# Priority for PSUM copies, gating and splits in an attention and gated-projection stage, and w_out decoded in four parts over four slots

## The chip, the cores and the metric

The kernel runs on one core of one Trainium2 chip. The metric is the device time of one execution in microseconds (us). TensorE is called PE (its weight loads PEld), VectorE DVE, ScalarE ACT, GpSimd POOL, and SyncE, which issues most transfers, SP.

## The reference

Three layers are computed one after the other in float32 (8 batches, 8 heads, 576 tokens, head size 64, so 4608 tokens of 512 features):

```python
# attention within chunks of 64 tokens
scores = scale * q_c @ k_c.T; attn = softmax(scores); x = attn @ v_c      # heads side by side: (B, S, 512)
# gated projection
gate = sigmoid(sum_k conv_w[k] * x shifted by k)                         # 5 taps along the tokens
x = (gate * (x @ w_val)) @ w_out
# feed-forward with layer norm
xn = (x - mu) / sqrt(var + 1e-6) * g_ln
out = x + relu(xn @ w_ch1) @ w_ch2
```

The weights arrive as float64, so the kernel decodes them from pairs of 32-bit words. Each float32 product is made of three matmuls on a high and a low part (hi*hi, hi*lo, lo*hi).

## The kernel before

**Units and blocks.** Attention goes by 36 units of 128 tokens, the gated projection by nine blocks of 512 tokens (four units). `slot(u)` writes, in this order: the loads of unit u+2 on SP, `a1(u)` (transposes of k and q on PE into two PSUM buffers of the pool `ps_t`, each copied out by ACT as `kT` and `qT`), the dense work of the slot's first half, `a4(u-2)` (transposes of the softmax result `pr`, copied out as `pT`), `a3(u)` (scores `sc` on PE; maximum `mx`, difference `ex`, sum `sm`, reciprocal and product `pr` on DVE, the exponential on ACT), `a5(u-2)` (product with v into `x`; ACT copies it twice, as `xf` and as the high part `xh`; POOL makes the low part `xl`), and the dense work of the second half.

**Dense work of a block.** `conv` makes the gate's argument `cg` (one ACT pass and four DVE passes per feature tile), `sigm` takes one sigmoid over the whole block on ACT, with a table load before it and another when the exponential comes back. `val(j, f)` runs twelve matmuls into `psv`, one of two PSUM buffers of the pool `ps_d`. DVE multiplies it with the gate into `gv`, which frees the buffer, ACT rounds `gv` to the high part `gh`, DVE takes the low part `gl`. `proj(j, t)` runs twelve matmuls on `gh`, `gl` and the split of w_out (`oh`, `ol`) into `pso`, which ACT copies to `y` and sends to DRAM. I call the four `val` chains of a block V#1 to V#4. V#3 needs the buffer that the `gv` of V#1 frees.

**Decode.** `split_w("o")` decodes w_out in four pieces: an ACT pass (line 107), three DVE passes (lines 108, 109, 110; the tile `da`, of which there are three), the high part on ACT (line 115) and the low part on POOL (line 116). It is written in slot 5. The feed-forward weights go the same way later (`split_ff`, called by `prep` after the last slot), some of them early, in gaps of the attention stage.

**What sets the order.** Each engine works through its own queue in order. A scheduler orders these queues when the program is built: work that is written earlier has the better priority, and work with nothing in its way is pulled forward into gaps. Only PE is kept in written order, in slots 0 to 6 and in the second half of the feed-forward.

Of the kernel before, what the change touches and what calls it, by code (L numbers as in the profile page):

```python
# [19 lines left out]
def tile_chunk_attention_gated_mlp(ctx: ExitStack, tc: tile.TileContext, q, k, v, w_val, conv_w, w_out, g_ln, w1, w2, out):  # L20
    nc = tc.nc
# [15 lines left out]
    CT = DM // P  # L37
# [28 lines left out]
    pD1 = s_d.enter_context(tc.tile_pool(name="pD1", bufs=1))  # L66
# [8 lines left out]
    y_dram = [dram.tile([BLK, DM], F32, name=f"yd{j}") for j in range(NB)]  # L75
# [36 lines left out]
    def split(hi, lo, raw, pool=None):  # L112
        a = (pool or stg).tile([P, DM], F32, tag="da", name="da", bufs=3)
        decode(raw, a)
        nc.scalar.activation(out=hi, in_=a, func=ACTF.Copy)
        nc.gpsimd.tensor_tensor(out=lo, in0=a, in1=hi, op=ALU.subtract)
        return a

    wv = {}

    def load_w(w, nm, slot0):
        raws = []
        for c in range(CT):
            raw = wA.tile([P, DM, 2], U32, tag=f"s{slot0 + c}", name="raw")
            nc.sync.dma_start(out=raw, in_=w[c * P:(c + 1) * P])
            raws.append(raw)
        wv[nm] = raws

    def split_w(nm):
        hs, ls = [], []  # L130
        for c, raw in enumerate(wv[nm]):
            hi = pD1.tile([P, DM], F32R, name=f"{nm}h{c}")
            lo = pD1.tile([P, DM], F32R, name=f"{nm}l{c}")
            split(hi, lo, raw)
            hs.append(hi)
            ls.append(lo)
        wv[nm] = (hs, ls)

    w1s, w2s, wraw = {}, {}, {}

# [29 lines left out]
    kT, qT, pt, pT = {}, {}, {}, {}  # L170

    def transpose_in(u, src, dst, nm):
        a = src.pop(u)
        t = pA.tile([P, NP, UN], F32, tag=nm, name=nm)
        ps = ps_t.tile([P, NP, UN], F32, tag="t", name="pst")
        for hp in range(NP):
            nc.tensor.transpose(out=ps[:, hp, :], in_=a[:, hp].rearrange("p r d -> p (r d)"), identity=ident)
        nc.scalar.activation(out=t, in_=ps, func=ACTF.Copy)
        dst[u] = t

    def a1(u):
        transpose_in(u, kr, kT, "kT")
        transpose_in(u, qr, qT, "qT")
# [30 lines left out]
    def a4(u):  # L214
        pr = pt.pop(u)
        t = pA.tile([P, NP, P], F32, tag="pT", name="pT")
        ps = ps_t.tile([P, NP, P], F32, tag="t", name="pst")
        for hp in range(NP):
            nc.tensor.transpose(out=ps[:, hp, :], in_=pr[:, hp].rearrange("p r k -> p (r k)"), identity=ident)
        nc.scalar.activation(out=t, in_=ps, func=ACTF.Copy)  # L220
        pT[u] = t

    xf, xh, xl = {}, {}, {}

    def new_block(j):
        o = boundary(j)
        t = pD2.tile([P, CT, BLK + 2 * HALO], F32, tag="xf", name="xf")
        if j == 0:
            nc.gpsimd.memset(t[:, :, 0:HALO], 0.0)
        else:  # L230
            ob = boundary(j - 1)
            e = BLK + (HALO if ob < BLK else 0)
            nc.gpsimd.tensor_copy(out=t[:, :, 0:HALO], in_=xf[j - 1][:, :, e:e + HALO])
        if o < BLK:
            nc.gpsimd.memset(t[:, :, HALO + o:2 * HALO + o], 0.0)
        xf[j] = t
        xh[j] = pD2.tile([P, CT, BLK], F32R, tag="xh", name="xh")
        xl[j] = pD2.tile([P, CT, BLK], F32R, tag="xl", name="xl")

    def a5(u):  # L240
        t = pT.pop(u)
        j, uu = divmod(u, UPB)
        va = vr.pop(u)
        x = ps_x.tile([P, 2, NP, UN], F32, tag="x", name="x")
        for i in range(NP // 2):
            for c in range(2):
                for f in range(2):
                    for r in range(2):
                        r0, o0 = CH * r, CH * f
                        nc.tensor.matmul(  # L250
                            out=x[o0:o0 + CH, r, i, c * CH:(c + 1) * CH],
                            lhsT=va[r0:r0 + CH, c, 2 * i + f, :],
                            rhs=t[r0:r0 + CH, 2 * i + f, c * CH:(c + 1) * CH],
                            start=True, stop=True,
                        )
        x = x[:, :, 0:NP // 2, :]
        if uu == 0:
            new_block(j)
        o = boundary(j)
        a, b = uu * UN, (uu + 1) * UN  # L260
        segs = [(max(a, lo), min(b, hi), sh) for lo, hi, sh in ((0, o, HALO), (o, BLK, 2 * HALO)) if max(a, lo) < min(b, hi)]
        for lo, hi, sh in segs:
            dst = xf[j][:, :, lo + sh:hi + sh].rearrange("p (r i) t -> p r i t", r=2)
            nc.scalar.activation(out=dst, in_=x[:, :, :, lo - a:hi - a], func=ACTF.Copy)
        for lo, hi, sh in segs:
            src = xf[j][:, :, lo + sh:hi + sh]
            dst = xh[j][:, :, lo:hi].rearrange("p (r i) t -> p r i t", r=2)
            nc.scalar.activation(out=dst, in_=x[:, :, :, lo - a:hi - a], func=ACTF.Copy)  # L268
            nc.gpsimd.tensor_tensor(out=xl[j][:, :, lo:hi], in0=src, in1=xh[j][:, :, lo:hi], op=ALU.subtract)  # L269


    cg = pD1.tile([P, CT, BLK + HALO], F32, name="cg")
# [17 lines left out]
    gh, gl = {}, {}  # L290

    def chain(ps, ops):
        n = len(ops)
        for i, (lt, rh) in enumerate(ops):
            nc.tensor.matmul(out=ps, lhsT=lt, rhs=rh, start=(i == 0), stop=(i == n - 1))  # L295

    def val(j, f):
        hs, ls = wv["v"]
        fs = slice(f * P, (f + 1) * P)
        ps = ps_d.tile([P, BLK], F32, tag="d", name="psv")  # L300
        ops = []
        for c in range(CT):
            ops += [(hs[c][:, fs], xh[j][:, c, :]), (hs[c][:, fs], xl[j][:, c, :]), (ls[c][:, fs], xh[j][:, c, :])]
        chain(ps, ops)
        o = boundary(j)
        gv = pD2.tile([P, BLK], F32, tag="gv", name="gv")
        for lo, hi, sh in ((0, o, 0), (o, BLK, HALO)):
            if lo < hi:
                nc.vector.tensor_tensor(out=gv[:, lo:hi], in0=ps[:, lo:hi], in1=cg[:, f, lo + sh:hi + sh], op=ALU.mult)  # L309
        a = pD1.tile([P, BLK], F32R, tag=f"gh{f}", name="gh")  # L310
        b = pD1.tile([P, BLK], F32R, tag=f"gl{f}", name="gl")
        nc.scalar.activation(out=a, in_=gv, func=ACTF.Copy)  # L312
        nc.vector.tensor_tensor(out=b, in0=gv, in1=a, op=ALU.subtract)  # L313
        gh[j, f], gl[j, f] = a, b

    def proj(j, t):
        hs, ls = wv["o"]
        ts = slice(t * P, (t + 1) * P)
        ps = ps_d.tile([P, DM], F32, tag="d", name="pso")
        ops = []  # L320
        for f in range(CT):
            ops += [(gh[j, f][:, ts], hs[f]), (gh[j, f][:, ts], ls[f]), (gl[j, f][:, ts], hs[f])]
        chain(ps, ops)
        y = pD2.tile([P, DM], F32, tag="y", name="y")
        nc.scalar.activation(out=y, in_=ps, func=ACTF.Copy)
        nc.scalar.dma_start(out=y_dram[j][ts, :], in_=y)

# [321 lines left out]
    def at(u, pos, fn):  # L651
        dense.setdefault((u + pos[0], pos[1]), []).append(fn)

    for j in range(NB):
        u = UPB * (j + 1) + LAG - 1
# [9 lines left out]
        for t in range(BLK // P):  # L665
            at(u, [(4, 0), (4, 1), (5, 0), (6, 0)][t], lambda j=j, t=t: proj(j, t))
    at(0, (4, 1), lambda: load_w(w_out, "o", CT))
    at(0, (5, 1), lambda: split_w("o"))
    for u in range(3, NU + LAG + 6):
        if u == MANUAL:  # L670
            head.close()
# [43 lines left out]
    for s in range(NS):  # L715
        for p in range(NPR):
# [3 lines left out]
            if s + 1 < NS and 2 <= p < 6:  # L720
                i = 2 * (p - 2)
# [30 lines left out]
```

## Time and profile before

| what | value |
|---|---|
| median of 3 runs | 1196.09 us (1195.82 to 1197.68) |
| the profiled execution | 1193.61 us, of which its span 1191.8 us |
| busy share of PE, DVE, ACT, POOL | 94%, 62%, 44%, 13% |
| mean granted clock of PE | 0.977 of 2.4 GHz |

The page gives shares over the whole span; the attention and projection stage takes the first 380 us of it, and a change there is read from the rows of that stage. A row of the timeline gives the start, the duration, the engine, the line, the operation and its tiles, and in brackets how long the engine had been idle and what ended that.

### The profile page before, as it was taken

Reading aid. Unit: us, or ns where it says so; the run is one execution under the profiler, and the core shown is the slowest. Engines: PE = TensorE matmul, PEld = TensorE weight load, DVE = VectorE, ACT = ScalarE, POOL = GpSimd, SP = SyncE. Lnnn points to the kernel's source line nnn. Section 1 sums busy time; section 2 is a strip of 40 time slices with the busy share of each in tenths; the row PEclk is TensorE's granted clock in tenths of the full one; section 3 lists DMA queues with packets and bytes.
Section 4 is the critical chain, followed back from the end, with each engine's and each line's share of the span. In section 5 each row is a group of like instructions: output and inputs, shape, how many; then the busy total and the mean of one; then the engine's idle time right before and its main releaser. Section 6 shows DMA issues by size and latency. Waiting matters only on the chain.

```text
span 1191.8 us, 18298 instructions
## 1 busy us (share of the span) xinstructions
PE 1114.5 (94%) x7128; PEld 902.3 (76%) x7128; DVE 738.2 (62%) x1237; ACT 527.4 (44%) x972; POOL 158.1 (13%) x160
## 2 busy tenths in 40 slices
PE   7859999899999688789999999999999999999998
PEld 6747777777777566568888878888788887878876
DVE  6878899988894985644564753534835436442433
ACT  4557678676666564333443323332413424221221
POOL 2221133111211433322221000000000000000000
PEclk8979999999999999989999999999999999999999
DMA  7655676655113673233333353332532332622212
GB/s 182 172 114 131 166 190 182 176 148 131 45 63 126 213 248 119 98 133 124 142 124 106 126 194 105 106 124 89 198 120 89 124 106 98 223 86 89 89 36 79
DMA packets 168860, 155.37 MB, mean 130 GB/s; under 512 B 120622, under 2 KB 128838, under 8 KB 168774
## 3 DMA queue, kind: packets, MB, share of 16 engines
q1 hardware_dynamic: 163590, 144.76, 39.7%
q10 hardware_dynamic: 5184, 9.44, 2.1%
q8 instruction: 56, 0.92, 0.3%
q14 instruction: 30, 0.25, 0.1%
HBM read 116.41 MB, written 37.75 MB: 129 GB/s over the span
## 4 chain that ended last, share of the span: by engine, by line
PE 61%; DVE 26%; ACT 5%; issue 3%; SPq 2%; DMA 1%; POOL 1%; DVEq 0%; POOLq 0%; ACTq 0%
PE acc L501 14%; PE x L526 14%; PE psf L501 14%; PE zy L526 9%; DVE cg L281 8%; PE psv L295 3%; DVE da L109 2%; DVE pr L211 2%; DVE da L110 2%; PE pso L295 2%; DVE sm L208 2%; PE psh L295 2%; DVE ex L202 1%; PE pst L369 1%; DVE mx L199 1%
## 5 line engine op out<-in xcount | busy, mean ns | idle before, releaser
L544 DVE TENSOR_TENSOR c<-x,c 128x512 f32<-128x512 f32 x96 | 66.1, 689 | 231.5 <-ACT c L540 175.1
L501 PE MATMUL acc<-w,h 128*128 128x512 f32 x768 | 186.0, 391 | 0.0
L501 PE MATMUL psf<-w,h 128*128 128x512 f32 x768 | 186.0, 391 | 0.0
L501 PEld LDWEIGHTS acc<-w,h 128*128 128x128 f32 x768 | 144.2, 188 | 31.4
L501 PEld LDWEIGHTS psf<-w,h 128*128 128x128 f32 x768 | 144.2, 188 | 31.3
L526 PE MATMUL x<-t,wc 128*128 128x512 f32 x576 | 149.4, 395 | 4.6 <-DVE c L544 4.2
L540 ACT ACTIVATE c<-zy 128x512 f32<-128x512 f32 x96 | 57.9, 603 | 195.2 <-PE zy L526 195.2
L526 PEld LDWEIGHTS x<-t,wc 128*128 128x128 f32 x576 | 109.3, 190 | 29.6 <-DVE c L544 5.1
L535 ACT ACTIVATE h<-c 128x512 fp32r<-128x512 f32 x96 | 60.5, 631 | 135.8 <-DVE c L544 135.2
L281 DVE SCALAR_TENSOR_TENSOR cg<-xf,cw,cg 128x516 f32<-128x516 f32 (+1 forms) x176 | 116.3, 707 | 0.8 <-ACT cg L279 0.6
L506 DVE TENSOR_TENSOR yt<-psf,yt 128x512 f32<-128x512 f32 x128 | 88.0, 689 | 23.8 <-PE psf L501 19.7
L526 PE MATMUL zy<-b,wc 128*128 128x512 f32 x384 | 100.1, 397 | 0.0
L526 PEld LDWEIGHTS zy<-b,wc 128*128 128x128 f32 x384 | 72.1, 190 | 14.9
L536 DVE SCALAR_TENSOR_TENSOR h<-c,h 128x512 fp32r<-128x512 f32 x96 | 68.0, 709 | 13.1 <-ACT h L535 12.7
L269 POOL TENSOR_TENSOR xl<-xf,xh 128x512 fp32r<-128x512 f32 (+1 forms) x40 | 50.3, 1260 | 154.1 <-ACT xh L268 153.9
L295 PE MATMUL psv<-xh,vh 128*128 128x512 f32 x144 | 60.3, 419 | 7.1 <-DVE gv L309 6.1
L411 POOL TENSOR_TENSOR wc<-raws,wc 128x256 fp32r<-128x256 f32 x56 | 48.4, 885 | 132.5 <-ACT wc L410 132.4
L295 PE MATMUL pso<-oh,gh 128*128 128x512 f32 x144 | 60.1, 417 | 5.6 <-ACT gh L312 5.1
L295 PE MATMUL psv<-xl,vh 128*128 128x512 f32 x144 | 57.5, 399 | 0.9 <-POOL xl L269 0.9
L295 PE MATMUL pso<-oh,gl 128*128 128x512 f32 x144 | 56.9, 397 | 0.7 <-DVE gl L313 0.7
L295 PE MATMUL psv<-xh,vl 128*128 128x512 f32 x144 | 57.4, 398 | 0.0
L526 PE MATMUL zy<-t,wc 128*128 128x512 f32 x192 | 50.6, 399 | 7.0 <-ACT t L410 3.9
(114 smaller groups left out, 1777.7 us busy)
## 6 DMA issues: line engine op xcount, KB each, us to landing
wc<-wc SPq DMA_DIRECT2D x112, 512.0 KB, 3.2
raw<-in_moe_w_ch SPq DMA_DIRECT2D x32, 512.0 KB, 5.0
yr<-yd SPq DMA_DIRECT2D x48, 256.0 KB, 3.0
vr<-in_v SPq DMA_DIRECT2D x144, 64.0 KB, 2.6
yd<-y ACTq DMA_DIRECT2D x36, 256.0 KB, 2.5
kr<-in_k SPq DMA_DIRECT2D x64, 128.0 KB, 2.9
qr<-in_q SPq DMA_DIRECT2D x64, 128.0 KB, 3.0
out<-yt SPq DMA_DIRECT2D x20, 256.0 KB, 3.1
```

The source lines that it names most:

```text
L109: nc.vector.scalar_tensor_tensor(out=au, in0=hw, scalar=0x80000000, in1=au, op0=ALU.bitwise_and, op1=ALU.bitwise_or)
L269: nc.gpsimd.tensor_tensor(out=xl[j][:, :, lo:hi], in0=src, in1=xh[j][:, :, lo:hi], op=ALU.subtract)
L281: nc.vector.scalar_tensor_tensor(out=o, in0=x[:, f, i + lo:i + hi], scalar=cw[:, i * CT + f:i * CT + f + 1], in1=o, op0=ALU.mult, op1=ALU.add,
L295: nc.tensor.matmul(out=ps, lhsT=lt, rhs=rh, start=(i == 0), stop=(i == n - 1))
L411: eng.tensor_tensor(out=lo, in0=a, in1=hi, op=ALU.subtract)
L501: nc.tensor.matmul(out=ps, lhsT=lt, rhs=rh, start=(g == 0 and k == 0 and (first or half)), stop=(g == 1 and k == 2 and (last or half)),)
L506: nc.vector.tensor_tensor(out=yt[i], in0=ps, in1=yt[i], op=ALU.add)
L526: nc.tensor.matmul(out=ps, lhsT=lt, rhs=rh, start=(start and c == 0 and i == 0), stop=(c == 1 and i == 2), skip_group_check=True)
L535: nc.scalar.activation(out=t[:, 0, :], in_=src, func=ACTF.Relu)
L536: nc.vector.scalar_tensor_tensor(out=t[:, 1, :], in0=src, scalar=0.0, in1=t[:, 0, :], op0=ALU.max, op1=ALU.subtract)
L540: nc.scalar.activation(out=t, in_=zy, func=ACTF.Copy)
L544: nc.vector.tensor_tensor(out=t, in0=x, in1=t, op=ALU.add)
```

## The change

The copies of `kT`, `qT`, `pT`, the whole of `xf`/`xh`/`xl`, the gating (`gv`, `gh`, `gl`) and the copy and transfer of `y` are written inside `tc.high_priority()`, so that the scheduler takes them before other work that is ready. `split_w` takes a range of pieces, and the four pieces of w_out are asked for in slots 5, 6, 7 and 8 instead of all in slot 5.

```diff
-    def split_w(nm):
-        hs, ls = [], []
-        for c, raw in enumerate(wv[nm]):
+    def split_w(nm, c0=0, c1=CT):
+        hs, ls = wv.setdefault(nm + "s", ([], []))
+        for c, raw in list(enumerate(wv[nm]))[c0:c1]:
...
     def transpose_in(u, src, dst, nm):
...
-        nc.scalar.activation(out=t, in_=ps, func=ACTF.Copy)
-        dst[u] = t
+        with tc.high_priority():
+            nc.scalar.activation(out=t, in_=ps, func=ACTF.Copy)
+            dst[u] = t
...
     def a5(u):
...
+        with tc.high_priority():
+            for lo, hi, sh in segs:
...
+                nc.scalar.activation(out=dst, in_=x[:, :, :, lo - a:hi - a], func=ACTF.Copy)
...
     def val(j, f):
...
+        with tc.high_priority():
+            for lo, hi, sh in ((0, o, 0), (o, BLK, HALO)):
+                if lo < hi:
+                    nc.vector.tensor_tensor(out=gv[:, lo:hi], in0=ps[:, lo:hi], in1=cg[:, f, lo + sh:hi + sh], op=ALU.mult)
...
+            nc.scalar.activation(out=a, in_=gv, func=ACTF.Copy)
+            nc.vector.tensor_tensor(out=b, in0=gv, in1=a, op=ALU.subtract)
...
     def proj(j, t):
...
+        with tc.high_priority():
+            nc.scalar.activation(out=y, in_=ps, func=ACTF.Copy)
+            nc.scalar.dma_start(out=y_dram[j][ts, :], in_=y)
...
-    at(0, (5, 1), lambda: split_w("o"))
+    for c in range(CT):
+        at(0, (5 + c, 1), lambda c=c: split_w("o", c, c + 1))
```

Where DVE's queue comes to the end of the convolution of block 0 (`cg` is that convolution, `da` the decode of w_out, `sm` and `pr` the softmax). Before, up to the last `cg`:

```order
L110 SCALAR_TENSOR_TENSOR da<-raw,da 128x512
L109 SCALAR_TENSOR_TENSOR da<-raw,da 128x512
L208 TENSOR_REDUCE sm<-ex_143 128x8
L110 SCALAR_TENSOR_TENSOR da<-raw,da 128x512
L209 RECIPROCAL sm<-sm 128x8
L281 SCALAR_TENSOR_TENSOR cg<-xf,cw,cg 128x256
L211 TENSOR_TENSOR pr<-ex_143,sm 128x512
L281 SCALAR_TENSOR_TENSOR cg<-xf,cw,cg 128x256
L199 TENSOR_REDUCE mx<-sc 128x8
L281 SCALAR_TENSOR_TENSOR cg<-xf,cw,cg 128x256
L202 TENSOR_TENSOR ex_144<-sc,mx 128x2x4x64
L281 SCALAR_TENSOR_TENSOR cg<-xf,cw,cg 128x256
```

And in the changed kernel, on the same engine around the last `cg` of block 0 and on to the first `gv`:

```order
L283 SCALAR_TENSOR_TENSOR cg<-xf,cw,cg 128x256
L108 TENSOR_SCALAR da<-da 128x512
L283 SCALAR_TENSOR_TENSOR cg<-xf,cw,cg 128x256
L208 TENSOR_REDUCE sm<-ex_143 128x8
L283 SCALAR_TENSOR_TENSOR cg<-xf,cw,cg 128x256
L209 RECIPROCAL sm<-sm 128x8
L109 SCALAR_TENSOR_TENSOR da<-raw,da 128x512
L211 TENSOR_TENSOR pr<-ex_143,sm 128x512
L110 SCALAR_TENSOR_TENSOR da<-raw,da 128x512
L108 TENSOR_SCALAR da<-da 128x512 x2
L109 SCALAR_TENSOR_TENSOR da<-raw,da 128x512 x2
L312 TENSOR_TENSOR gv<-psv,cg 128x512 x2
```

Before, all twelve decode passes of w_out stand ahead of the last `cg`. Now four do (one piece and the first pass of the second), six stand between it and the first `gv`, and the last two after that.

ACT's queue at the same place, before (`cg` at line 288 is the sigmoid of block 0):

```order
L107 ACTIVATE da<-raw 128x512
L206 ACTIVATE ex_143<-ex_143 128x8x64
L178 ACTIVATE kT<-pst 128x512
L115 ACTIVATE oh_762<-da 128x512
L178 ACTIVATE qT<-pst 128x512
L220 ACTIVATE pT<-pst 128x512
L115 ACTIVATE oh_771<-da 128x512
L264 ACTIVATE xf<-x 128x4x128
L268 ACTIVATE xh<-x 128x4x128
L206 ACTIVATE ex_144<-ex_144 128x8x64
L288 ACT_TABLE_LOAD
L288 ACTIVATE cg<-cg 128x4x512
```

And in the changed kernel, from the same pass of the decode on:

```order
L107 ACTIVATE da<-raw 128x512
L206 ACTIVATE ex_143<-ex_143 128x8x64
L178 ACTIVATE kT<-pst 128x512
L290 ACT_TABLE_LOAD
L290 ACTIVATE cg<-cg 128x4x512
L178 ACTIVATE qT<-pst 128x512
L221 ACTIVATE pT<-pst 128x512
L115 ACTIVATE oh_859<-da 128x512
L315 ACTIVATE gh<-gv 128x512 x2
L115 ACTIVATE oh_991<-da 128x512
L266 ACTIVATE xf<-x 128x4x128
L178 ACTIVATE kT<-pst 128x512
```

The sigmoid moved ahead of seven passes, among them the exponential of the next unit.

ACT's queue around the sigmoid of a later block (block 2), before:

```order
L288 ACT_TABLE_LOAD
L288 ACTIVATE cg<-cg 128x2064
L206 ACT_TABLE_LOAD
L206 ACTIVATE ex_144<-ex_144 128x8x64
L312 ACTIVATE gh<-gv 128x512
L264 ACTIVATE xf<-x 128x4x128
L268 ACTIVATE xh<-x 128x4x128
L312 ACTIVATE gh<-gv 128x512
L178 ACTIVATE kT<-pst 128x512
L178 ACTIVATE qT<-pst 128x512
L220 ACTIVATE pT<-pst 128x512
```

And in the changed kernel:

```order
L290 ACT_TABLE_LOAD
L290 ACTIVATE cg<-cg 128x2064
L266 ACTIVATE xf<-x 128x4x128
L270 ACTIVATE xh<-x 128x4x128
L206 ACT_TABLE_LOAD
L206 ACTIVATE ex_144<-ex_144 128x8x64
L178 ACTIVATE kT<-pst 128x512
L178 ACTIVATE qT<-pst 128x512
L315 ACTIVATE gh<-gv 128x512 x2
L221 ACTIVATE pT<-pst 128x512
```

The same ten passes stand ahead of `pT`, but `xf`, `xh`, `kT` and `qT` now come before both `gh`. From the last projection of block 8 on, no engine's queue differs.

## Rows read from the trace of the kernel before

**Rows 1.** Busy time by stage: us, PE, PEld, DVE, ACT, POOL, PEclk, DMA

```profile
48.00:84.00 36.00, 22.17 (x258) 17.36 (x258) 29.02 (x48) 20.19 (x37) 9.71 (x9) 0.72 0.68 170
84.00:345.00 261.00, 244.95 (x2823) 196.71 (x2823) 231.38 (x385) 185.05 (x306) 53.51 (x52) 0.99 0.51 134
...
400.00:465.00 65.00, 48.13 (x202) 38.01 (x202) 56.42 (x109) 39.04 (x89) 28.86 (x23) 0.92 0.66 215
```

**Rows 2.** Waits of PE in 48 to 84 us: total, times, longest

```profile
PE pst L219 <- ACT kT L178: 10.2, 2, 6.4
PE sc L192 <- ACT qT L178: 1.8, 1, 1.8
```

**Rows 3.** Timeline of PE, 77 to 87 us, first and last matmuls of V#3 and V#4

```profile
77.27 0.78 PE L295 MATMUL psv<-xh,vh 128*128 128x512 f32 x1
...
82.01 0.39 PE L295 MATMUL psv<-xh,vl 128*128 128x512 f32 x1
...
83.82 0.50 PE L295 MATMUL psv<-xh,vh 128*128 128x512 f32 x1
...
86.47 0.39 PE L295 MATMUL psv<-xh,vl 128*128 128x512 f32 x1
```

**Rows 4.** Timeline of DVE, 54 to 77 us

```profile
54.64 0.68 DVE L199 TENSOR_REDUCE mx<-sc 128x8 f32<-128x512 f32 x1
...
58.06 0.41 DVE L108 TENSOR_SCALAR da<-da 128x512 uint32<-128x512 uint32 x1
58.40 0.68 DVE L110 SCALAR_TENSOR_TENSOR da<-raw,da 128x512 uint32<-128x512 uint32 x1
59.00 0.68 DVE L109 SCALAR_TENSOR_TENSOR da<-raw,da 128x512 uint32<-128x512 uint32 x1
...
60.00 1.75 DVE L110 SCALAR_TENSOR_TENSOR da<-raw,da 128x512 uint32<-128x512 uint32 x1
...
72.21 0.47 DVE L281 SCALAR_TENSOR_TENSOR cg<-xf,cw,cg 128x256 f32<-128x256 f32 x1
...
73.71 0.20 DVE L209 RECIPROCAL sm<-sm 128x8 f32<-128x8 f32 x1
73.95 0.69 DVE L211 TENSOR_TENSOR pr<-ex,sm 128x512 f32<-128x512 f32 x1
76.20 1.29 DVE L309 TENSOR_TENSOR gv<-psv,cg 128x512 f32<-128x512 f32 x2 [1.56 <-ACT cg L288]
```

**Rows 5.** Timeline of POOL, the low part of the first w_out piece

```profile
59.82 1.38 POOL L116 TENSOR_TENSOR ol<-da,oh 128x512 fp32r<-128x512 f32 x1 [2.56 <-ACT oh L115]
```

**Rows 6.** Timeline of ACT, 63 to 76 us

```profile
63.38 0.58 ACT L178 ACTIVATE kT<-pst 128x512 f32<-128x512 f32 x1
...
72.97 1.28 ACT L288 ACT_TABLE_LOAD   x1
74.26 1.91 ACT L288 ACTIVATE cg<-cg 128x2048 f32<-128x2048 f32 x1
```

**Rows 7.** Busy time from one block's sigmoid start to the next, columns as rows 1

```profile
74.26:109.93 35.67, 32.86 (x384) 26.89 (x385) 25.82 (x41) 22.72 (x36) 4.08 (x4) 0.89 0.40 102
109.93:145.70 35.77, 34.34 (x403) 27.50 (x402) 29.83 (x50) 24.92 (x41) 5.92 (x6) 1.00 0.67 168
145.70:183.70 38.00, 35.05 (x398) 27.77 (x397) 36.75 (x60) 28.86 (x50) 11.60 (x11) 0.96 0.70 180
...
220.50:257.32 36.82, 33.69 (x401) 27.30 (x400) 34.06 (x58) 25.13 (x43) 5.62 (x7) 1.00 0.64 172
```

**Rows 8.** Waits of PE in 84 to 345 us: total, times, longest

```profile
PE psv L295 <- DVE gv L309: 6.1, 4, 2.8
PE pso L295 <- ACT gh L312: 4.8, 5, 2.1
PE pst L219 <- ACT kT L178: 2.1, 4, 0.6
```

**Rows 9.** Timeline of ACT, `pT` in the slot after the sigmoid of block 1

```profile
117.05 0.60 ACT L220 ACTIVATE pT<-pst 128x512 f32<-128x512 f32 x1 [0.26 <-PE pst L219]
```

More of the change, by code (lines that the diff above doesn't have):

```diff
@@ L136, in split_w @@
             ls.append(lo)
-        wv[nm] = (hs, ls)
     w1s, w2s, wraw = {}, {}, {}
@@ L219, in a4 @@
             nc.tensor.transpose(out=ps[:, hp, :], in_=pr[:, hp].rearrange("p r k -> p (r k)"), identity=ident)
-        nc.scalar.activation(out=t, in_=ps, func=ACTF.Copy)
-        pT[u] = t
+        with tc.high_priority():
+            nc.scalar.activation(out=t, in_=ps, func=ACTF.Copy)
+            pT[u] = t
     xf, xh, xl = {}, {}, {}
@@ L261, in a5 @@
         segs = [(max(a, lo), min(b, hi), sh) for lo, hi, sh in ((0, o, HALO), (o, BLK, 2 * HALO)) if max(a, lo) < min(b, hi)]
[L262 to L269, printed above, removed]
+        with tc.high_priority():
+            for lo, hi, sh in segs:
+                dst = xf[j][:, :, lo + sh:hi + sh].rearrange("p (r i) t -> p r i t", r=2)
+                nc.scalar.activation(out=dst, in_=x[:, :, :, lo - a:hi - a], func=ACTF.Copy)
+            for lo, hi, sh in segs:
+                src = xf[j][:, :, lo + sh:hi + sh]
+                dst = xh[j][:, :, lo:hi].rearrange("p (r i) t -> p r i t", r=2)
+                nc.scalar.activation(out=dst, in_=x[:, :, :, lo - a:hi - a], func=ACTF.Copy)
+                nc.gpsimd.tensor_tensor(out=xl[j][:, :, lo:hi], in0=src, in1=xh[j][:, :, lo:hi], op=ALU.subtract)
     cg = pD1.tile([P, CT, BLK + HALO], F32, name="cg")
@@ L297, in val @@
     def val(j, f):
-        hs, ls = wv["v"]
+        hs, ls = wv["vs"]
         fs = slice(f * P, (f + 1) * P)
@@ L306, in val @@
         gv = pD2.tile([P, BLK], F32, tag="gv", name="gv")
[L307 to L313, printed above, removed]
+        with tc.high_priority():
+            for lo, hi, sh in ((0, o, 0), (o, BLK, HALO)):
+                if lo < hi:
+                    nc.vector.tensor_tensor(out=gv[:, lo:hi], in0=ps[:, lo:hi], in1=cg[:, f, lo + sh:hi + sh], op=ALU.mult)
+            a = pD1.tile([P, BLK], F32R, tag=f"gh{f}", name="gh")
+            b = pD1.tile([P, BLK], F32R, tag=f"gl{f}", name="gl")
+            nc.scalar.activation(out=a, in_=gv, func=ACTF.Copy)
+            nc.vector.tensor_tensor(out=b, in0=gv, in1=a, op=ALU.subtract)
         gh[j, f], gl[j, f] = a, b
     def proj(j, t):
-        hs, ls = wv["o"]
+        hs, ls = wv["os"]
         ts = slice(t * P, (t + 1) * P)
@@ L324, in proj @@
         y = pD2.tile([P, DM], F32, tag="y", name="y")
-        nc.scalar.activation(out=y, in_=ps, func=ACTF.Copy)
-        nc.scalar.dma_start(out=y_dram[j][ts, :], in_=y)
+        with tc.high_priority():
+            nc.scalar.activation(out=y, in_=ps, func=ACTF.Copy)
+            nc.scalar.dma_start(out=y_dram[j][ts, :], in_=y)
     p2 = {}
```

## Prediction

> **What bounds the kernel now.** I read the busy time by stage first. From 84 to 345 us PE is busy 244.95 of 261 us, so there PE itself is the limit and at most 16 us can be won. Just before, from 48 to 84 us, PE is busy only 22.17 of 36 us and is granted 0.72 of 2.4 GHz, while DVE is busy 29.02 [rows 1]. That is the one place of the stage with a large hole. The list of waits names it: PE stands 10.2 us in two gaps, the longer 6.4, before the transposes of `pr`, because a `ps_t` buffer has not been emptied by the copy `kT` [rows 2]. V#3 starts right after the second gap, at 77.27 [rows 3]. The copy is not slow (0.58 us); it stands in ACT's queue behind the sigmoid, which runs from 74.26 to 76.17 [rows 6]. The sigmoid needs the last `cg`, which DVE finishes at 72.21 + 0.47 = 72.68, and V#3 needs the sigmoid too, through the first `gv` at 76.20 [rows 4]. So the end of the hole is set by DVE's queue ahead of the last `cg`, and in that queue stand all twelve decode passes of w_out. A second stretch is not PE-bound: from 400 to 465 us PE is busy 48.13 of 65 us and DVE 56.42 [rows 1].
>
> **The change part by part.** The instructions are the same in number and kind; only their order moves.
>
> *The first sigmoid.* In the changed order, from the first decode pass to the last `cg`, DVE has one L109 and one L110 (0.68 each), two L108 (0.41), `mx`, `ex` and `sm` (0.68 each, by the `mx` row) and six `cg` (0.47) [rows 4]: 1.36 + 0.82 + 2.04 + 2.82 = 7.0 us. It starts at 55.3, where DVE was through with the earlier `cg` and the `mx` (54.64 + 0.68); the `mx` now comes later, but the exponential before it also does. That gives 62.3. Two things can add to it. The exponential stands on ACT behind the fourth L107, which needs the `da` tile that POOL's first `ol` frees. And a DVE pass beside a POOL pass can grow: the L110 at 60.00 took 1.75 instead of 0.68 us while POOL worked from 59.82 to 61.20 [rows 4, 5]. I allow 0.7 us for the two together: the last `cg` ends at 63, with bounds 62 and 64.4 (two such passes), against 72.68.
>
> ACT can load the table meanwhile, so the sigmoid (1.91) ends near 65 [rows 6]. But DVE first does what now stands between: a reciprocal and `pr` (0.20 + 0.69), two L108, and four passes of L109 and L110, 0.9 + 0.82 + 2.72 = 4.4 us [rows 4]. So `gv` starts at 67.4, its first half takes 0.65 [rows 4], and V#3 can start at 68, or at 69.1 if one more pass meets POOL. Before it started at 77.27 [rows 3].
>
> From V#3 to V#4 before, 83.82 - 77.27 = 6.55 us went by, of which 82.40 - 77.27 = 5.1 were V#3 itself [rows 3]. Now `x`, which stands between the two, waits for `pT`, and `pT` stands on ACT behind both `gh`, two parts of the w_out split, five copies and exponentials (eight passes of 0.58), a table load (1.28) and another exponential [rows 6]. From the first `gv` on that is 4.6 + 1.3 + 0.6, and 0.6 for `pT` itself: 68 + 7.1 = 75.1. With `x`, some half of the 1.4 us that were left between V#3 and V#4, V#4 starts at 76. Against 83.82 this is a **gain of 7.8 us**. The bounds: 10 if V#3 and what ACT does behind it go at the best of these rows (V#4's matmuls are 0.24 us apart, V#3's 0.43 [rows 3]) and nothing holds `pT`; 4 if three further DVE passes meet POOL (3 x 1.07). What hides the moved passes: in the block after the first sigmoid DVE is idle for 35.67 - 25.82 = 9.85 us [rows 7], and the decode passes now behind the last `cg` cost 0.82 + 6 x 0.68 = 4.9. If that cover were gone, they would cost 4.9 us.
>
> On the clock: V#3's matmuls were spaced at 0.43 us behind the 6.4 us gap, V#4's at 0.24 [rows 2, 3]. The Trainium skill (TensorE: Matmul & The Clock Gate, HAM oscillation) says that idle gaps of PE throttle it, and that it stays at full rate if they are kept short. The trace agrees as far as its one long gap goes. By that rule the shorter gaps of the new order could leave V#3 at 2.4 GHz, and the gain would be nearer to 10 than to 7.8.
>
> *Slots 3 to 7.* `xh` moves ahead of the exponential, and the transposes of `pr` ahead of V#1. PE may reach the end of V#2 some 1 us earlier or later, but then it waits for `kT` all the same. I count 0, bounds -1 and +1.
>
> *The later blocks.* A block without much decode takes 35.8 us with PE busy 34.3 [rows 7]. Its waits are PE on `kT` before the transposes, up to 0.6 us, and PE on `gh` before the last projection steps, 4.8 us in five [rows 8]. `kT` now precedes both `gh`, so its wait goes. But `pT` stays where it was: it came 117.05 - (109.93 + 1.91) = 5.2 us behind the end of the sigmoid [rows 6, 7, 9], and the same ten passes still stand ahead of it, so `x` waits there instead. What is left is a shorter way from `gv` to `gh`, of which I take a third of the two waits of rows 8: (4.8 + 2.1) / 3, a **gain of 2** over seven blocks. Bounds: 0, if `pT` takes all of it, and 6.9, both waits in full.
>
> *Blocks with feed-forward decode.* There DVE is full (36.75 of 38.0 us) [rows 7], and V#3 waited for `gv`, 6.1 us in four places [rows 8]. Now the first two `gv` stand ahead of the last decode pass, 0.68 us [rows 4]; in three blocks that is 2 us. But on ACT a part of that split now stands between `gh` and `pT`, one pass of 0.58 per block [rows 6], 1.7 us. A **gain of 0.3**, bounds a gain of 6.1 and a loss of 4 (two queued passes of 0.68 in each of three blocks).
>
> *The end of the stage.* The second `xn` on ACT now stands behind the second `y`, which ends 24 matmuls of 0.24 us, 5.8 us, before the feed-forward's first matmul can start; with the two passes of DVE behind it, it fits. 0, bounds -1 and +1. Behind that all queues are alike. The feed-forward's later decode can begin only when the projection's tiles are free, so it starts earlier by what is won.
>
> *The sum.* 7.8 + 2 + 0.3 = 10.1 us. The profiled execution took 1193.61, so it would take 1183.5. The median of the runs is 2.5 us above the profiled one, so I forecast a median of **1186.0**.
>
> **The rivals.**
> - *Handed back.* The lead is lost again where DVE is the limit, from 400 to 465 us (56.42 of 65 us busy) [rows 1]. For it: DVE has the same work in all. Against it: the work there waits for tiles that come free with the projection, and 9.85 us of idle DVE lie at hand much earlier [rows 7]. Time: 1193.7 to 1197, no change.
> - *Only half.* The order does not spread the decode over four slots (six passes still stand between the last `cg` and the first `gv`), and V#3 is held by passes that meet POOL. It takes the lower bound of 4 and nothing from the blocks: 1192.
> - *`pT` behind the gating (slower).* In every block `pT` now waits in ACT's queue behind two `gh`, hence behind two `gv`, hence behind what DVE does before them. If that holds `x` for two copies and one decode pass more than reckoned, 2 x 0.58 + 0.68 = 1.8 us [rows 4, 6], in eight blocks, it costs 14.7 us against the 10.1 won: +4.6, so 1200.7. It decides from 1.3 us per block on. Against it: in a block without decode `pT` stands where it stood.
> - *More.* The waits of rows 8 nearly all go: 7.8 + 10 us, 1178.
>
> **How the numbers follow.** Forecast 0.56 (1182 to 1190.5), only half 0.12, handed back 0.14, slower 0.10, more 0.08. A difference under 0.2%, 2.4 us, can't be told from none here. Faster: 0.56 + 0.12 + 0.08 = 0.76. Same 0.14, slower 0.10. The range leaves out the slower case, the upper part of "handed back" and the lower half of "more": 1179 to 1194.5.
>
> **What would show it.** In the changed trace the first sigmoid should start near 63 and V#3 near 68, V#4 near 76; PE's waits on `kT` in the first 84 us should fall from 10.2 us to some 4. From one sigmoid to the next blocks should take 35.3 to 36.8 us. The feed-forward's first matmul should come 10 us earlier. It would be wrong if V#4 starts after 80, if waits of `x` on `pT` of a us or more appear in each block, or if the stretch with DVE as the limit grows by what was won.

## The result, and the profile after

The changed kernel takes **1182.87 us** in the median of four runs (1181.95 to 1183.74), the kernel before 1195.95 us on the same chip (1195.3 to 1197.68). The ratio is 0.9888, 95% interval 0.9871 to 0.9905: 13.1 us, or 1.1%, faster. The forecast was 1186.0, range 1179.0 to 1194.5. The profiled execution took 1183.74 us (span 1182.0), where the sum of the prediction gave 1183.5. That the sum met it so closely is partly chance, as the second traces below show. In a second set of runs, below, the medians are 11.6 us apart.

The stages first, columns as in [rows 1], whose lines these answer; the third is taken 10 us earlier, since the changed kernel is about that far ahead there:

```profile
48.00:84.00 36.00, 27.15 (x320) 21.54 (x324) 30.10 (x54) 25.11 (x45) 11.76 (x10) 0.86 0.73 183
84.00:345.00 261.00, 246.68 (x2809) 198.32 (x2801) 228.27 (x393) 183.43 (x306) 54.16 (x52) 0.99 0.53 139
390.00:455.00 65.00, 49.33 (x201) 38.64 (x200) 57.36 (x111) 38.19 (x84) 31.01 (x23) 0.89 0.66 217
```

From 48 to 84 us PE now works 27.15 us, where it was 22.17. The waits of PE in this stretch, against [rows 2]:

```profile
PE pst L219 <- ACT kT L178: 2.6, 2, 2.3
PE sc L192 <- ACT qT L178: 2.6, 1, 2.6
PE x L251 <- ACT pT L221: 1.6, 1, 1.6
```

The 10.2 us of waiting for `kT` are 2.6, and a wait of `x` for `pT` is new. The steps around the first sigmoid, against [rows 3, 4, 6]; the timelines of DVE, ACT and PE, in this order:

```profile
61.83 0.48 DVE L283 SCALAR_TENSOR_TENSOR cg<-xf,cw,cg 128x256 f32<-128x256 f32 x1
...
65.97 1.28 DVE L312 TENSOR_TENSOR gv<-psv,cg 128x512 f32<-128x512 f32 x2
```

```profile
62.98 1.91 ACT L290 ACTIVATE cg<-cg 128x2048 f32<-128x2048 f32 x1
...
71.88 1.28 ACT L206 ACT_TABLE_LOAD   x1
73.17 0.63 ACT L206 ACTIVATE ex<-ex 128x512 f32<-128x512 f32 x1
73.71 0.58 ACT L221 ACTIVATE pT<-pst 128x512 f32<-128x512 f32 x1
```

```profile
65.43 1.14 PE L192 MATMUL sc<-kT,qT 64*64 64x64 f32 x32 [2.59 <-ACT qT L178]
...
68.11 0.60 PE L297 MATMUL psv<-xh,vh 128*128 128x512 f32 x1
...
74.34 0.70 PE L251 MATMUL x<-pT,vr 64*64 64x64 f32 x32 [1.59 <-ACT pT L221]
74.96 0.61 PE L297 MATMUL psv<-xh,vh 128*128 128x512 f32 x1
...
79.18 0.39 PE L297 MATMUL psv<-xh,vl 128*128 128x512 f32 x1
```

V#3 starts at 68.11 (77.27 before) and V#4 at 74.96 (83.82). But from the first of V#4's twelve matmuls to the last it now takes 79.18 - 74.96 = 4.22 us, where it was 86.47 - 83.82 = 2.65. Next, from one sigmoid's start to the next, against [rows 7]:

```profile
62.98:102.56 39.58, 35.24 (x455) 29.30 (x456) 33.64 (x53) 27.03 (x44) 10.01 (x8) 0.89 0.52 128
102.56:137.28 34.72, 33.81 (x401) 27.36 (x400) 28.10 (x49) 24.15 (x39) 5.63 (x6) 1.00 0.64 159
137.28:173.49 36.21, 34.20 (x402) 27.46 (x401) 32.39 (x56) 27.88 (x47) 8.69 (x9) 1.00 0.68 173
173.49:210.73 37.24, 34.14 (x401) 27.38 (x400) 33.64 (x58) 27.53 (x46) 10.25 (x9) 1.00 0.65 172
210.73:251.42 40.69, 36.35 (x400) 29.16 (x400) 36.87 (x61) 28.11 (x48) 11.54 (x11) 0.92 0.65 169
251.42:286.63 35.21, 34.21 (x402) 27.51 (x401) 30.79 (x54) 24.25 (x39) 5.50 (x5) 1.00 0.62 158
286.63:321.46 34.83, 33.95 (x402) 27.45 (x401) 28.09 (x49) 24.22 (x41) 5.76 (x6) 1.00 0.19 54
```

Blocks with little decode take 34.7 to 35.2 us, and one block takes 40.69. The waits of PE in 84 to 345 us, against [rows 8]:

```profile
PE psv L297 <- DVE gv L312: 3.4, 4, 1.1
PE pso L297 <- ACT gh L315: 3.3, 5, 1.2
PE pso L297 <- DVE gl L316: 3.0, 3, 1.8
PE x L251 <- ACT pT L221: 2.3, 4, 0.8
```

The waits for `gv`, `gh` and `kT`, 6.1, 4.8 and 2.1 us before, are 3.4, 3.3 and none. Waits for `gl` and `pT` have come in their place; before, they were 0.5 and 0.4.

To follow the gain I use the start of each block's sigmoid on ACT. Starts in us, from the timelines; "again" is a second trace of the same kernel, from an experiment below. Blocks 1 to 4 lie between the second and the sixth sigmoid:

| kernel | 1st sigmoid | end of V#4 | 2nd | 6th | 8th | 9th | first matmul of the feed-forward | end of span |
|---|---|---|---|---|---|---|---|---|
| before | 74.3 | 86.9 | 109.9 | 257.3 | 328.4 | 354.9 | 378.6 | 1191.8 |
| before, again | 73.0 | 85.4 | 108.4 | 259.1 | 330.2 | 356.6 | 380.4 | 1193.7 |
| changed | 63.0 | 79.6 | 102.6 | 251.4 | 321.5 | 346.9 | 368.7 | 1182.0 |
| changed, again | 63.8 | 78.8 | 102.4 | 250.1 | 320.1 | 345.6 | 367.4 | 1179.9 |
| spread alone | 62.2 | 77.8 | 101.0 | 250.1 | 321.3 | 349.2 | 372.9 | 1187.0 |
| priority alone | 69.6 | 81.1 | 104.1 | 252.1 | 321.7 | 347.1 | 370.6 | 1184.5 |

With two traces of each, the mean lead of the changed kernel is 6.7 us at the second sigmoid, 7.4 at the sixth, 8.5 at the eighth, 11.5 at the feed-forward's first matmul and 11.8 at the end. So over half is won in block 0, little in blocks 1 to 4, and another 4 us from the sixth sigmoid to the end of the stage.

### The profile page after: what moved, and what is told of

It is laid out like the page before. It is cut to its first block, busy times and chain, and to the rows that moved or that the text cites. A ratio compares the mean times of both kernels' runs of the same rounds, so it can differ in the third digit from the quotient of the medians.

```text
span 1182.0 us, 18293 instructions
## 1 busy us (share of the span) xinstructions
PE 1113.3 (94%) x7128; PEld 901.9 (76%) x7128; DVE 728.8 (62%) x1237; ACT 526.8 (45%) x972; POOL 160.5 (14%) x160
## 4 chain that ended last, share of the span: by engine, by line
PE 61%; DVE 22%; ACT 6%; DMA 4%; issue 4%; SPq 3%; POOL 1%; DVEq 0%; ACTq 0%; POOLq 0%
PE acc L505 14%; PE x L530 14%; PE psf L505 13%; PE zy L530 9%; DVE cg L283 6%; PE psv L297 2%; PE pso L297 2%; DVE da L109 2%; PE psh L297 2%; PE pst L373 1%; DVE da L110 1%; DVE h L540 1%; DVE sm L208 1%; DVE pr L211 1%; SPq L89 1%
## 5 line engine op out<-in xcount | busy, mean ns | idle before, releaser
L510 DVE TENSOR_TENSOR yt<-psf,yt 128x512 f32<-128x512 f32 x128 | 88.0, 690 | 23.8 <-PE psf L505 19.8
L540 DVE SCALAR_TENSOR_TENSOR h<-c,h 128x512 fp32r<-128x512 f32 x96 | 68.1, 709 | 13.1 <-ACT h L539 12.7
L271 POOL TENSOR_TENSOR xl<-xf,xh 128x512 fp32r<-128x512 f32 (+1 forms) x40 | 50.6, 1269 | 147.8 <-ACT xh L270 147.7
L116 POOL TENSOR_TENSOR w<-da,w 128x512 fp32r<-128x512 f32 x32 | 47.6, 1496 | 87.0 <-ACT w L115 86.8
```

Of the source, the lines that this page charges most:

```text
L510: nc.vector.tensor_tensor(out=yt[i], in0=ps, in1=yt[i], op=ALU.add)
L540: nc.vector.scalar_tensor_tensor(out=t[:, 1, :], in0=src, scalar=0.0, in1=t[:, 0, :], op0=ALU.max, op1=ALU.subtract)
```

## Experiments

The times are medians in us, each beside runs of the kernel before on the same chip.

### Each half of the change alone

`spread_alone` leaves the priorities out, at all five places:

```diff
-        with tc.high_priority():
+        if True:
             nc.scalar.activation(out=t, in_=ps, func=ACTF.Copy)
```

> Only the second half of the change: w_out is asked for in four slots, and no copy, gating or split has priority. Theory one (the gain of the changed kernel is the first sigmoid, and the spread alone makes it): the first sigmoid starts at 63 as in the changed kernel, V#4 of block 0 at 75 to 77, and the blocks without feed-forward decode take 35.7 us as before, so that of the 13.1 us about 1 to 2 are missing: 1184 to 1186. Theory two (the priorities carry the gain in every block, and the lead of the first sigmoid is handed back): 1190 or more, with the first sigmoid no later than 65.

`priority_alone` takes the spread back:

```diff
-    for c in range(CT):
-        at(0, (5 + c, 1), lambda c=c: split_w("o", c, c + 1))
+    at(0, (5, 1), lambda: split_w("o"))
```

> Only the first half of the change: priority for the copies, gating and splits, and w_out asked for in one slot as before. Theory one: the decode passes still stand ahead of the last cg, the first sigmoid starts at 72 to 74 and V#4 at 83 to 84; only the 0.8 to 1 us per block without decode is won, so the lead at the feed-forward's first matmul is 2 to 4 us and the time 1192 to 1194.5. Theory two: 1188 or less, with blocks of 34.7 us wherever there is no decode.

Measured: spread alone **1188.47** against 1196.74 (ratio 0.9921, 0.9902 to 0.994); priority alone **1186.07** (0.99, 0.9879 to 0.9921). By the times, theory one fell in both. Theory two holds for the priority alone (1188 or less, and 34.7 to 34.9 us per block without decode); neither gives the time of the spread alone. Alone, the spread wins 8.3 us and not 11 to 12, and the priority wins 10.7 and not 2 to 4. Together they win 11.6 to 13.1, less than the 19 of the sum, so the two halves overlap. The interval of the priority alone overlaps that of the whole change, so the times don't show that the spread adds anything to it.

The table shows where. The spread alone puts the first sigmoid at 62.2 and is 7.4 to 8.9 us ahead at the second. Behind the eighth sigmoid its trace loses 1.4 us, 349.2 - 321.3 = 27.9 instead of 26.5; PE's mean granted clock there was 0.94, and 1.00 in the kernel before. `ff_plain_before` below, which has neither half, shows the same 27.9 at 0.94. The last stretch to the feed-forward, 372.9 - 349.2, takes 23.7 us as before. The priority alone moves the first sigmoid too, to 69.6, which I had not expected, and V#4 ends at 81.1: it ends 7.3 us earlier than before in the changed kernel, 5.7 with the priority alone and 9.0 with the spread alone. The waits of PE from 48 to 84 us, with the priority alone and then with the spread alone:

```profile
PE pst L219 <- ACT kT L178: 7.5, 3, 3.7
```

```profile
PE pst L219 <- ACT kT L178: 5.6, 1, 5.6
```

Each half shortens the same wait of [rows 2], which was 10.2, and a hole can be closed only once.

### Which priority

`copy_priority` keeps it for `kT`, `qT`, `pT`, `xf`, `xh`, `xl`, `gating_priority` for `gv`, `gh`, `gl`; both keep the spread. The edits are the one of the first diff, at the other places.

> The spread over four slots and priority only for kT, qT, pT, xf, xh and xl, not for gv, gh, gl and y. Theory one (a block without decode is 0.8 us shorter because kT comes ahead of gh): blocks 5 to 7 take 34.8 us and the time is within 1.5 us of the changed kernel's, some 1182 to 1185. Theory two (the gating's priority shortens them): 35.5 us per block, 1187 to 1189 like the spread alone.

> The spread over four slots and priority only for gv, gh and gl. Theory one: kT still comes behind both gh, blocks 5 to 7 take 35.5 us, the time is 1186 to 1189. Theory two: 34.8 us per block, 1182 to 1185.

Measured: copies **1182.52** (0.9883, 0.9865 to 0.9901), gating **1185.96** (0.9907, 0.989 to 0.9924), against 1195.8. The times agree with theory one, but its reason does not: with the gating's priority alone a block without decode takes 34.8 us too (sigmoids at 285.2 and 320.0). The intervals of the two overlap, and their traces (spans of 1179.8 and 1181.2) don't part them. Either way is enough to shorten a block. PE's waits from 257 to 328 us, two blocks without decode, before and then in the changed kernel:

```profile
PE pst L219 <- ACT kT L178: 1.3, 2, 0.6
PE pso L295 <- ACT gh L312: 0.9, 2, 0.5
```

```profile
PE psv L297 <- DVE gv L312: 0.7, 1, 0.7
PE x L251 <- ACT pT L221: 0.4, 1, 0.4
PE pso L297 <- ACT gh L315: 0.4, 2, 0.2
```

Twice 0.6 us for `kT` became one wait of 0.4 for `pT`, and the waits for `gh` halved; a wait of 0.7 for `gv` is new. In all, 2.2 us of waits became 1.5.

### The new wait for pT in block 0

`late_priority` gives the priorities only from slot 9 on, so that in block 0 `pT` stands between the two `gh`, as with the spread alone:

```diff
-        with tc.high_priority():
+        with tc.high_priority() if u + LAG >= 9 else nullcontext():
             nc.scalar.activation(out=t, in_=ps, func=ACTF.Copy)
             pT[u] = t
```

> The spread over four slots, and the priorities only from slot 9 on, so that block 0 has the order of the run with the spread alone (pT between the two gh) and the later blocks that of the changed kernel. Theory one (in block 0 the priorities cost: in the changed kernel x waits 1.59 us for pT behind both gh, and V#4 ends at 79.6, against 77.8 with the spread alone; what is won there lasts): V#4 ends near 77.8, the blocks without decode take 34.8 us, the lead at the feed-forward's first matmul is 11 to 12 us, and the time is 1.5 to 2 us under that of the changed kernel. Theory two (the lead of block 0 is handed back where feed-forward weights are decoded, since the kernels so far all stand 5.2 to 7.2 us ahead at the sixth sigmoid, whatever they won before): that sigmoid comes at 250 to 252 again, and the time is within 1 us of the changed kernel's.

`changed_again` is the changed kernel, unchanged.

> The changed kernel once more, on the same chip as the three others: 1182 to 1184 if the chips agree. All theories expect the same; its second trace shows how far the leads at the sigmoids and the last 700 us differ between two executions of one program.

Measured: **1183.59** and **1184.25** (0.9893 and 0.9892, the latter 0.9875 to 0.9909). The time is that of theory two: no difference. But neither mechanism was put to the test, since block 0 won nothing: V#4 ended at 79.2 and not at 77.8, and the second sigmoid came at 102.3, as in the changed kernel (102.6, 102.4). The edit also takes the priority of `kT` in block 0 away. PE then stands 6.2 us in one wait for `kT`, and no longer for `qT` and `pT`; in the changed kernel the three waits are 2.6 + 2.6 + 1.6 = 6.8 us. So these traces show no gain of the priorities in block 0 on top of the spread. What the wait for `pT` costs by itself is not shown.

The second trace of the changed kernel showed something else. PE at the same place in it:

```profile
75.19 0.69 PE L251 MATMUL x<-pT,vr 64*64 64x64 f32 x32 [1.40 <-ACT pT L221]
75.82 0.50 PE L297 MATMUL psv<-xh,vh 128*128 128x512 f32 x1
...
78.44 0.39 PE L297 MATMUL psv<-xh,vl 128*128 128x512 f32 x1
```

Here V#4 takes 2.62 us from its first matmul to its last, against 4.22 in the first trace. The 4 us from 76 to 80, the first trace and then the second:

```profile
76.00:80.00 4.00, 4.00 (x17) 3.21 (x16) 3.93 (x6) 0.82 (x2) 1.28 (x1) 0.67 0.66 148
```

```profile
76.00:80.00 4.00, 4.00 (x22) 3.38 (x23) 3.93 (x7) 2.31 (x5) 1.30 (x1) 1.00 0.66 150
```

PE is busy all the time in both. In the first it is granted 0.67 of 2.4 GHz and gets through 17 matmuls, in the second 1.00 and 22.

### Filling the gap on PE

`fill_gaps` has PE run idle matmuls ahead of one unit's scores, to keep the clock up for V#3 and V#4:

```diff
+        for _ in range(FILL if u == UPB + LAG + 1 else 0):
+            nc.tensor.matmul(out=sc[:, 0, NP:NP + 2, :], lhsT=kt[:, 0, :], rhs=ident, start=True, stop=True)
```

> The changed kernel with seven idle 128-column matmuls into an unused part of the scores' buffer, which PE runs in the gap of 2.59 us ahead of the scores at 65.43 us. Theory one (the low clock in block 0 comes from that gap): the granted clock from 62 to 84 us rises from 0.78 to 0.9 or more, V#3 and V#4 each take 3 us, V#4 ends at 78 or earlier, and the second sigmoid comes 1 to 2 us before 102.4: 1181 to 1183. Theory two (the filler delays what is behind it, or the clock falls in the next gap anyway): V#4 ends at 79 or later, 1183 to 1185.

Measured: **1184.69** (0.9912, 0.9889 to 0.9934), no better. The stretch from 62 to 84 us in the second trace of the changed kernel, and with the filler:

```profile
62.00:84.00 22.00, 17.16 (x224) 13.68 (x224) 18.34 (x30) 16.89 (x27) 7.24 (x6) 0.84 0.66 148
```

```profile
62.00:84.00 22.00, 19.49 (x210) 16.66 (x210) 18.00 (x30) 15.79 (x25) 7.20 (x6) 0.84 0.65 146
```

The mean clock was 0.84, above the 0.78 of the changed kernel's first trace and the same as in its second, so no gain of the filler is shown. V#4 ended at 80.1, since it ran at the low clock again, behind the next gap, in which `x` waits for `pT`:

```profile
74.86 0.69 PE L254 MATMUL x<-pT,vr 64*64 64x64 f32 x32 [1.70 <-ACT pT L224]
```

The time and V#4's end are those of theory two. The scores behind the filler started at 66.5; the copy `qT` that they need had ended at 65.9, so the filler itself cost 0.6 us there.

### The decode of w_out without its DVE passes

`w_out_no_dve_passes` leaves lines 108 to 110 out for w_out.

> The changed kernel without the three DVE passes that decode w_out (its high and low part are then made from the undecoded high words, so the output is another). Twelve passes of DVE, 7.1 us, are gone from around the first sigmoid. Theory one (DVE's queue still sets when V#3 and V#4 start): the first sigmoid comes about 2 us earlier, V#3 3 to 4 us earlier, V#4 at 71 to 73, 1179 to 1181. Theory two (ACT's queue, with pT behind both gh, sets when x and V#4 come): V#4 stays within 1 us of 75, 1182 to 1184.

Measured: **1185.52** (0.9901, 0.988 to 0.9921). This is inconclusive, since the scheduler built another order from it: all four `oh` passes stand ahead of the sigmoid and `kT` behind it, the sigmoid came at 64.8, PE waited 5.87 us for that `kT`, and V#4 ended at 80.0. DVE ended the last `cg` at 63.9, later than in the changed kernel (62.3) although it had fewer passes, and ACT's table load, behind the four `oh`, ended only at 64.8. So fewer passes on DVE did not bring the sigmoid forward in this order.

### Feed-forward decode in blocks 1 to 4

`ff_decode_even` spreads the decode of the first four feed-forward tiles over slots 11 to 25:

```diff
+    for f in range(NFA):
+        at(0, (11 + 4 * f - 1, 1), lambda f=f: load_ff(f, stg))
+        for part in range(2):
+            at(0, (11 + 4 * f + 2 * part, 1), lambda f=f, part=part: split_ff(f, stg, part))
```

> The changed kernel, with the first four feed-forward tiles asked for in slots 11 to 25, a half every second slot, so that one, three, two, two and three pieces are decoded in blocks 1 to 5 where it was none, none, four, three and four. Theory one (in the changed kernel the block from 210.73 to 251.42 us lost 5 us because four pieces of decode meet the gating there, gl came late, PE stopped and its granted clock fell): that block takes 35 to 37 us and no other over 38, the lead at the feed-forward's first matmul grows by 2 to 5 us, 1178 to 1181. Theory two (the clock falls there by itself, or each piece costs the same wherever it stands): a block of 39 us or more remains or all grow alike, 1182 to 1184.

Measured: **1182.56** (0.9878, 0.9858 to 0.9899), the same as the changed kernel. No block over 37.5 us remained, yet blocks 1 to 4 took 36.1 + 37.3 + 36.7 + 37.5 = 147.6 us, 148.9 and 147.7 in the two traces of the changed kernel. (The expectation counts its blocks from the first sigmoid on; blocks 1 to 4 here have ten pieces instead of eleven.) That is theory two: a piece costs about the same wherever it stands.

`ff_plain_before` and `ff_plain_after` leave the three DVE passes of the feed-forward's decode out of each kernel:

```diff
-        decode(raw, a)
+        decode(raw, a, pool is None)
```

> The kernel before without the three DVE passes of each piece of feed-forward weight (the weights are then made from the undecoded high words). Theory one (in blocks 1 to 4 DVE's queue with the decode sets the pace, in both kernels): these four blocks take 35.6 us each, 142.4 in all instead of 147.4. Theory two (the loads, or the decode's passes on ACT and POOL, set it): 146 to 148 as before.

> The changed kernel with the same passes left out. Theory one: blocks 1 to 4 take 34.8 us each, 139.2 in all instead of 147.6 to 148.8, and the lead over the kernel before with the same omission is 12 to 14 us at the feed-forward's first matmul, where it was 9.9 and 11.2 with the decode. Theory two: 147 to 149, and the lead stays at 9 to 11.

Measured: **1175.3** and **1162.55**, 12.75 us apart, about as far as with the decode. Blocks 1 to 4 (from the second to the sixth sigmoid) took 147.4 and 150.7 us in the two traces of the kernel before, and 148.9 and 147.7 in those of the changed kernel. The first trace of each, then the two without the passes:

```profile
109.93:257.32 147.39, 137.44 (x1602) 110.69 (x1601) 135.56 (x226) 107.55 (x180) 34.01 (x34) 0.99 0.68 178
```

```profile
102.56:251.42 148.86, 138.50 (x1601) 111.35 (x1600) 131.00 (x221) 107.67 (x179) 36.11 (x35) 0.98 0.65 168
```

```profile
109.00:253.80 144.80, 136.86 (x1602) 109.14 (x1601) 120.19 (x193) 107.86 (x180) 36.85 (x34) 1.00 0.70 181
```

```profile
102.50:245.70 143.20, 135.85 (x1603) 109.51 (x1602) 117.09 (x193) 107.22 (x180) 35.82 (x34) 1.00 0.71 184
```

Theory one is right in its direction and too large. Without the passes the kernel before gains 2.6 to 5.9 us there and the changed kernel 4.5 to 5.7. The change then wins 1.6 us in these blocks instead of a mean of 0.8, but two executions of one kernel differ there by up to 3.3, so it is not shown that the decode takes back a part of what the priorities win. The lead at the feed-forward's first matmul is 376.6 - 362.5 = 14.1 us, the upper end of theory one. But 1.5 of it comes from the 27.9 us that `ff_plain_before` takes behind the eighth sigmoid, at the clock of 0.94. In the changed kernel blocks 1 to 4 take some 9 us more than four times 34.8; about 5 of them go with the passes, and the other 4 stay without a named cause.

### A second trace of the kernel before

> The kernel before once more, for a second trace. Its profiled execution of 1193.61 us lay 2.5 us below the median of its runs, that of the changed kernel did not. If single stretches with the granted clock at 1.2 GHz, such as the one from 514 to 523 us, come and go between executions, this trace shows one in another place or of another length, and the milestones up to the eighth sigmoid differ by less than 1 us from the first trace. If they don't, the stretch is there again, of the same length, and the time is 1193 to 1194.

Measured: 1196.31 (ratio to itself 1.0001, 0.9984 to 1.0019), the profiled execution 1195.54. The starts of its sigmoids differ by up to 1.8 us from the first trace, more than the 1 us that I expected. The low stretch in the feed-forward is there again, but shorter (from 518 to 521 us the granted clock was 0.60, from 521 on 1.00).

## Why the prediction was right, and where it was not

**The first sigmoid** (forecast 7.8, bounds 4 to 10). Up to the sigmoid the mechanism was as described: the last `cg` ended at 62.3 (forecast 63) and `gv` started at 66.0 (67.4). That V#3 then started at 68.1, as forecast (68), is partly luck. Its buffer was free when the first `gv` ended, near 66.6, but PE was still busy with what stands ahead of V#3, because the scores had waited 2.59 us for `qT`, whose copy stands on ACT behind the sigmoid. The forecast left that wait out. `x` waited for `pT`, as forecast, and V#4 started at 75.0 (76): 8.9 us earlier in the first pair of traces, 6.5 in the second (75.8 against 82.3). The step counted to V#4's start only; in the first trace 1.6 us more went in V#4's matmuls. At the second sigmoid the lead is 7.4 in the first pair and 6.0 in the second. The term is 6 to 7.4, inside its bounds. It is also not the spread's alone, as the halves show.

**The clock.** V#3 did come back to 2.4 GHz: from its first matmul to its last it took 3.18 us, with the transposes of `qr` between them, against 4.74 before. The result nearer to 10 did not come all the same. Where `x` waited for `pT`, V#4 followed at 1.2 GHz in three traces (after waits of 1.56, 1.59 and 1.70 us) and at 2.4 GHz in two (1.40 and 1.10 us). The Trainium skill (TensorE: Matmul & The Clock Gate, HAM oscillation) has it that idle gaps throttle PE and that it stays at full rate if they are kept short. The traces agree for the gap of 6.4 us before. For the short gaps three of these five traces do not, and whether the gap itself decided it is not shown.

**The later blocks** (forecast 2 over seven blocks, 0.3 each). The wait for `kT` went and `x` waits for `pT` instead, as forecast: 2.3 us in four waits from 84 to 345 us, the longest 0.8, where `kT` had taken 2.1. For a block without decode the size was off: I took a third of the waits of [rows 8], and such a block got 35.6 - 34.8 = 0.8 us shorter. Over all blocks the error hides: from the second to the ninth sigmoid the mean lead grows from 6.7 to 9.5 us, and this term and the next gave 2.3 together.

**Blocks with decode** (forecast a gain of 0.3, bounds +6.1 and -4). Blocks 1 to 4 took 147.4 and 150.7 us before, 148.9 and 147.7 after: a mean gain of 0.8, with 3.3 between two executions of one kernel. So no gain can be told there, and none of note was forecast. Two windows of [rows 7] miss the sigmoids, which start at 185.02 and 221.79: the block read as 38.0 us took 39.3, with DVE busy 38.1, and the one read as 36.8 took 35.5. That DVE is full in the first of them stands.

**The end of the stage** (forecast 0, bounds -1 and +1). This step failed. From the ninth sigmoid to the feed-forward's first matmul it took 23.7 and 23.8 us in the two traces before and 21.8 in both after: 2.0 us won. I looked only at `xn` and `y` on ACT, and not at `gh` of the last block. Before, two of them stood behind the layer norm of block 0:

```profile
362.64 3.17 ACT L371 ACTIVATE xt<-pst,cw 128x128 f32<-128x128 f32 x12
...
368.36 0.66 ACT L312 ACTIVATE gh<-gv 128x512 fp32r<-128x512 f32 x1
...
369.83 0.65 ACT L312 ACTIVATE gh<-gv 128x512 fp32r<-128x512 f32 x1
```

and PE waited for `y`, `gh` and `gl` in the last projection:

```profile
PE pso L295 <- ACT y L325: 0.5, 1, 0.5
PE pso L295 <- ACT gh L312: 0.4, 1, 0.4
PE pso L295 <- DVE gl L313: 0.2, 1, 0.2
```

In the changed kernel no wait of PE is listed between 346.9 and 368.7, and the `gh` stand between the norm's passes:

```profile
357.28 0.85 ACT L370 ACTIVATE yt<-yt,w,r 128x512 f32<-128x512 f32 x1
357.99 0.66 ACT L315 ACTIVATE gh<-gv 128x512 fp32r<-128x512 f32 x1
358.51 0.84 ACT L370 ACTIVATE yt<-yt,w,r 128x512 f32<-128x512 f32 x1
```

With priority for the copies only, these `gh` come behind twelve `xt` again, and the stretch takes 23.8 us. But early `gh` are not enough. With the priority alone they stand as in the changed kernel, and PE starts the projection's last matmul as early (21.6 us behind the ninth sigmoid, 21.5 in the changed kernel, 23.5 before). Yet the stretch takes 23.4 us, because the third `y` waits longer, by the profile for the transfer of an earlier `y`; the changed kernel, then the priority alone:

```profile
367.67 0.60 ACT L329 ACTIVATE y<-pso 128x512 f32<-128x512 f32 x1 [2.68 <-DMA yd<-y]
```

```profile
369.92 0.60 ACT L329 ACTIVATE y<-pso 128x512 f32<-128x512 f32 x1 [4.68 <-DMA yd<-y]
```

The feed-forward's first matmul then waits 1.5 us for that copy. The same wait is 1.1 us with the gating's priority alone, 1.8 in `w_out_no_dve_passes` and 2.3 in `ff_decode_even`. So the order wins 2 us here, and a late `y` can take most of it back; why the `y` is late in some traces stays open.

**The sum and the median.** 10.1 was forecast. The first pair of traces is 9.8 apart, the second 13.9, the medians 13.1 and 11.6 (in two sets of runs). So the sum was some 2 us short, about the end of the stage, and 1186.0 was 2 to 3 us too high. The first pair of traces hid that, by luck: the profiled execution of the kernel before lay 2.5 us under its median, that of the changed kernel 0.9 over its own. The 2.5 us that I added are no second slip; they only lead back to the median before, 1196.1.

**The rivals.** "Handed back" happened in a small part only: the mean lead of 11.5 us at the feed-forward's first matmul is 9.7 at the first matmul of its second half (493.6 and 497.1 before, 486.4 and 484.8 after); that it is 11.8 at the end goes with the clock, as the last section shows. In the stretch where DVE is the limit, DVE is busy 57.36 of 65 us in the changed kernel (from 390 to 455 us) and 56.42 before (from 400 to 465), so the stretch did not grow by what was won. "Only half" and "more" are both refuted by the times, and so is the slower case: `pT` behind the gating costs a wait of 1.59 us once and at most 0.8 us in a later block, under the 1.3 us per block from which it would decide.

## What to carry to other kernels

Two edits that close the same hole in the busy engine's time don't add up: before each is credited with its own gain, run each alone (here 8.3 and 10.7 us alone, 11.6 to 13.1 together). Where a priority moves one kind of instruction ahead everywhere, look for it at every place where the program changes stage, since there it meets other neighbours than in the steady blocks. Compare stretches of work, and not fixed windows of time, once one kernel is ahead of the other. And take two traces of each kernel before a term of 1 or 2 us is called confirmed.

## What was unexpected of the hardware

After a pause at the same place in the feed-forward, PE came back at either level of its clock. The 9 us behind that pause, in the kernel before (a pause of 3.38 us) and in the changed one (3.00 us), which there run the same instructions:

```profile
514.00:523.00 9.00, 8.21 (x23) 6.11 (x24) 3.79 (x6) 3.34 (x8) 1.41 (x2) 0.62 0.28 110
```

```profile
507.00:516.00 9.00, 8.19 (x34) 6.06 (x34) 4.86 (x7) 4.08 (x9) 2.87 (x4) 1.00 0.30 120
```

PE is equally busy, but gets through 23 matmuls at 0.62 and 34 at 1.00. From the feed-forward's second half to the end it took 698.0 to 698.2 us in the first trace of before and in those with the spread alone, the priority alone and `late_priority`, which also had the low stretch. It took 699.3 with the filler, where the stretch was longer, and 696.6 to 697.8 in the second trace of before, in `w_out_no_dve_passes` and in `ff_decode_even`, where it was shorter. And it took 695.1 to 695.6 in the two traces of the changed kernel and in those with the copies' or the gating's priority alone, which had none. That is some 2.6 us between kernels that run the same instructions there. The length of the pause alone does not decide it: the stretch came behind pauses of 2.43 to 3.40 us, and stayed away behind pauses of 3.00 to 3.06. What does stays open, and so does how much of it is in the medians.
